# Key and query loads in 1.5 KB rows, a turn of two tokens at a time, and work moved from VectorE to ScalarE, in a sparse-attention and Fourier kernel

## The chip, the cores and the metric

The kernel runs on one core of one Trainium2 chip, everything in float32. The metric is device time in microseconds (us), the median of the runs of one kernel. A run is "fast" when it is not more than 1.5% above the fastest of the same kernel; all runs used here are fast, except the single run of e1, whose state is unknown and whose time is not used. A ratio is the mean time of one kernel's fast runs over the mean of the fast runs of the kernel before in the same rounds on the same chip, so it is not quite the ratio of the medians that stand beside it. An interval is a 95% interval. PE is TensorE, DVE VectorE, ACT ScalarE, POOL GpSimd.

## The reference

Four batches, eight heads of 64 columns, 768 tokens. Each query sees the keys less than 16 tokens away, and 24 block summaries (the largest key and the mean value of each block of 32). The result goes through a two-dimensional Fourier transform and a channel part:

```python
k_sum = k.reshape(B, H, nb, 32, D).max(axis=3);  v_sum = v.reshape(B, H, nb, 32, D).mean(axis=3)
# softmax over [q.k / 8 where |i - j| < 16 , q.k_sum / 8 + log 32], times [v, v_sum]
x = attn_out.transpose(0, 2, 1, 3).reshape(B, S, 512)
u = x + np.real(np.fft.fft(np.fft.fft(x, axis=1), axis=2))
un = (u - mean(u)) / np.sqrt(var(u) + 1e-6)
out = u + np.maximum(un @ w_ch1, 0.0) @ w_ch2        # 512 -> 2048 -> 512
```

## The kernel before

The parts that the change touches. Two heads make a pair. Keys and queries of a pair are loaded head by head, one token of 64 columns (256 B) per row, then turned on PE so that the 128 partitions hold the columns of the two heads and the free axis holds the tokens:

```python
qn, kn = (apool.tile([P, NST, 2, D], FP, tag="nat", bufs=4, ...) for n in "qk")
for dst, src in ((kn, k), (qn, q)):
    for e in range(2):
        nc.sync.dma_start(out=dst[:, :, e, :], in_=src[b, 2 * g + e].rearrange("(t p) d -> p t d", p=P))
...
for src, dst in ((kn, kt[:, W:W + S]), (qn, qt)):
    for h in range(2):
        ps = abank([P, HT, P], ...)                      # one PSUM bank, HT = 3
        for i in range(HT):
            nc.tensor.transpose(ps[:, i, :], src[:, HT * h + i].rearrange("p e d -> p (e d)"), ident)
        nc.scalar.copy(out=dst[:, S2 * h:S2 * (h + 1)], in_=ps.rearrange("p i c -> p (i c)"))
```

In the Fourier part y is the first product; its copies, then mx (second product), statistics, normalisation and the turn of u follow, before the first channel product hx:

```python
nc.scalar.copy(out=ty[:, g, par:S2:2], in_=y[:, 0:F2])
nc.vector.tensor_copy(out=tr[:, g, par:S2:2], in_=ps[:, F2:0:-1])     # the reversed copy
...                                                                   # mx, statistics, 4 Newton steps
nc.vector.tensor_scalar(out=un[:, t, :], in0=x[:, t, :], scalar1=stat[:, i, 0:1], scalar2=y[:, i:i + 1],
                        op0=SUB, op1=ALU.mult)
...                                                                   # transposes into ps
(nc.scalar.copy if t % 2 else nc.vector.tensor_copy)(out=u[:, half:half + 3:2, :, P * i:P * (i + 1)], in_=ps)
```

The rectifier of the channel part is `nc.vector.tensor_scalar(out=t, in0=t, scalar1=0.0, ..., op0=ALU.max)`. Attention of batch b + 1 runs interleaved with the Fourier and channel part of batch b, so its turns stand in the same engine queues.

## Time and profile before

930.12 us, median of 3 runs (928.45 to 930.68). The prediction below shows the stages; here are the totals of the profile page (engine, busy us, share of the span, instructions):

```profile
PE 829.2 (89%) x6386; PEld 618.3 (67%) x6386; DVE 530.3 (57%) x1158; ACT 168.8 (18%) x349; POOL 147.4 (16%) x142
```

And the timeline of ACT beside the Fourier products of batch 1, start and duration in us. It shows a pair's turn copies: two of keys in 0.87 us and two of queries in 0.88 us (about 0.48 each):

```profile
361.90 0.87 ACT L591 COPY kt<-qk 128x384 f32<-128x384 f32 x2
362.64 0.88 ACT L591 COPY qt<-qk 128x384 f32<-128x384 f32 x2
363.87 0.34 ACT L792 COPY big<-y 128x192 f32<-128x192 f32 x1 [0.34 <-PE y L786]
```

For the comparison of stages I use one landmark, the start of the first y product of each batch, from the timeline: 80.4, 350.6, 549.0 and 744.6 us here, end 929.2. The stages between them are called batch 0's attention (80.4 us), batch 0 (270.2), batch 1 (198.4), batch 2 (195.6) and batch 3 (184.6). The "turn" of a batch is the time from its first y to its first hx: 38.7 us in batch 1, 38.9 in batch 2.

### The profile page before, as it was taken

What the parts mean: (1) busy time and instruction counts of PE and PEld (TensorE: products, weight loads), DVE (VectorE), ACT (ScalarE), POOL (GpSimd) and SP (SyncE); (2) the same over time, 40 slices, a digit from 0 to 9 for tenths busy, and PEclk for the clock granted to TensorE, in tenths of its full rate; (3) what the DMA queues carried; (4) which work ended last, traced back from release to release, by engine and by line L of the source; (5) the groups of instructions that cost most, each with busy time, mean ns of one, the idle gap of its engine ahead of it and who ended that gap; (6) DMA issues with size and microseconds to landing.
All of it is one profiled execution on the core that took longest, in us unless ns stands there. A gap on an engine that the chain in (4) does not pass through costs nothing.

```text
span 929.2 us, 15289 instructions
## 1 busy us (share of the span) xinstructions
PE 829.2 (89%) x6386; PEld 618.3 (67%) x6386; DVE 530.3 (57%) x1158; ACT 168.8 (18%) x349; POOL 147.4 (16%) x142
## 2 busy tenths in 40 slices
PE   4778748687886799999999999999999997999997
PEld 3656634466753588657875888668857875587586
DVE  1366986799368964935423937635327556352252
ACT  2222312432023102221112012220021011200200
POOL 2230625567056700020000000000000000000000
PEclk9777859989898999999999999999999998999999
DMA  9995791777926508826162147321051161213101
GB/s 187 178 189 164 236 178 62 219 228 218 163 76 244 199 35 287 151 97 147 35 206 78 57 150 232 86 80 41 27 197 60 46 261 54 105 41 153 45 24 48
DMA packets 127917, 122.76 MB, mean 132 GB/s; under 512 B 102912, under 2 KB 111328, under 8 KB 127840
## 3 DMA queue, kind: packets, MB, share of 16 engines
q1 hardware_dynamic: 127296, 121.14, 46.9%
q8 instruction: 52, 0.85, 0.4%
q10 hardware_dynamic: 544, 0.56, 0.2%
q14 instruction: 25, 0.20, 0.1%
HBM read 100.71 MB, written 20.97 MB: 131 GB/s over the span
## 4 chain that ended last, share of the span: by engine, by line
PE 68%; DVE 20%; DMA 4%; POOL 3%; issue 3%; SPq 2%; ACT 1%; DVEq 0%; ACTq 0%; POOLq 0%
PE ox L906 17%; PE hx L863 15%; PE oz L906 8%; PE hz L863 7%; PE oy L906 4%; PE hy L863 4%; PE y L786 3%; DMA raw<-in_moe_w_ch_dram 2%; DVE cvt L688 2%; POOL w L529 2%; DVE cvt L693 2%; PE sc L606 2%; DVE cvt L691 2%; DVE x L526 2%; DVE cvt L687 2%
## 5 line engine op out<-in xcount | busy, mean ns | idle before, releaser
L863 PE MATMUL hx<-u,w 128*128 128x384 f32 x512 | 189.2, 500 | 15.5 <-ACT h L876 6.0
L863 PEld LDWEIGHTS hx<-u,w 128*128 128x128 f32 x512 | 97.9, 195 | 85.8 <-ACT h L876 8.9
L906 PE MATMUL ox<-w,h 128*128 128x256 f32 x384 | 93.9, 393 | 8.4 <-DVE x L526 7.9
L863 PE MATMUL hz<-u,w 128*128 128x384 f32 x256 | 96.6, 498 | 4.7 <-ACT h L878 4.7
L906 PE MATMUL ox<-w,s 128*128 128x256 f32 x384 | 92.8, 384 | 4.0 <-DVE x L526 3.5
L906 PE MATMUL oz<-w,s 128*128 128x256 f32 x384 | 93.0, 384 | 2.6 <-DVE s L526 2.6
L906 PEld LDWEIGHTS ox<-w,h 128*128 128x128 f32 x384 | 75.4, 197 | 22.8 <-DVE x L526 9.1
L906 PEld LDWEIGHTS ox<-w,s 128*128 128x128 f32 x384 | 72.0, 191 | 16.3 <-DVE x L526 5.6
L526 DVE TENSOR_TENSOR x<-ox,x 128x256 f32<-128x256 f32 x96 | 40.4, 422 | 74.2 <-PE ox L906 74.2
L906 PEld LDWEIGHTS oz<-w,s 128*128 128x128 f32 x384 | 73.3, 192 | 13.1 <-DVE s L526 2.9
L863 PEld LDWEIGHTS hz<-u,w 128*128 128x128 f32 x256 | 49.8, 195 | 40.3 <-POOL vb L529 5.3
L529 POOL TENSOR_TENSOR w<-cvt 128x512 f32<-128x512 f32 x32 | 43.6, 1364 | 133.2 <-DVE cvt L693 72.5
L529 POOL TENSOR_TENSOR w<-w 128x256 f32<-128x256 f32 x64 | 56.2, 893 | 3.1
L526 DVE TENSOR_TENSOR h<-hy,h 128x384 f32<-128x384 f32 x32 | 17.8, 555 | 67.5 <-PE hy L863 67.5
L526 DVE TENSOR_TENSOR h<-hx,h 128x384 f32<-128x384 f32 x32 | 17.8, 555 | 56.1 <-PE hx L863 56.0
L863 PE MATMUL hy<-u,w 128*128 128x384 f32 x128 | 46.5, 486 | 0.0
L906 PE MATMUL oy<-w,h 128*128 128x256 f32 x192 | 46.0, 380 | 0.3 <-POOL w L529 0.3
L606 PEld LDWEIGHTS sc<-qt,kt 64*64 64x64 f32 x1536 | 33.7, 157 | 12.7 <-issue 8.6
L606 PE MATMUL sc<-qt,kt 64*64 64x32 f32 x1536 | 36.7, 239 | 6.0 <-issue 3.7
L906 PEld LDWEIGHTS oy<-w,h 128*128 128x128 f32 x192 | 36.5, 191 | 5.8 <-POOL w L529 0.7
L867 DVE TENSOR_SCALAR h<-h 128x384 f32<-128x384 f32 x96 | 38.7, 404 | 2.9
L526 DVE TENSOR_TENSOR s<-h 128x512 f32<-128x512 f32 x48 | 39.2, 816 | 0.2
(92 smaller groups left out, 1043.3 us busy)
## 6 DMA issues: line engine op xcount, KB each, us to landing
w<-dw SPq DMA_DIRECT2D x48, 896.0 KB, 5.6
raw<-in_moe_w_ch_dram SPq DMA_DIRECT2D x32, 512.0 KB, 5.1
dw<-w SPq DMA_DIRECT2D x16, 896.0 KB, 4.3
vw<-in_v_dram SPq DMA_DIRECT2D x62, 192.0 KB, 5.7
kn<-in_k_dram SPq DMA_DIRECT2D x32, 192.0 KB, 5.3
qn<-in_q_dram SPq DMA_DIRECT2D x32, 192.0 KB, 5.2
vb<-in_v_dram SPq DMA_DIRECT2D x16, 384.0 KB, 6.3
out_dram<-x SPq DMA_DIRECT2D x24, 256.0 KB, 2.0
```

What stands on the lines that cost most here:

```text
L526: nc.vector.tensor_tensor(out=out, in0=in0, in1=in1, op=op)
L529: nc.gpsimd.tensor_tensor(out=out, in0=in0, in1=in1, op=op)
L606: nc.tensor.matmul(ps[h][r:r + 64, i, :], kt[rows, o:o + 64], qt[rows, o:o + BLOCK], start=True, stop=True)
L687: nc.vector.tensor_scalar(out=ex, in0=high, scalar1=0x7FF00000, scalar2=None, op0=ALU.bitwise_and)
L688: nc.vector.tensor_scalar(out=man, in0=high, scalar1=0x000FFFFF, scalar2=None, op0=ALU.bitwise_and)
L691: nc.vector.scalar_tensor_tensor(out=ex, in0=high, scalar=-(1 << 31), in1=ex, op0=ALU.bitwise_and, op1=ALU.bitwise_or)
L693: nc.vector.scalar_tensor_tensor(out=tmp[:, 1, :], in0=low, scalar=2.0 ** -52, in1=tmp[:, 1, :], op0=ALU.mult, op1=ALU.add)
L786: nc.tensor.matmul(y, fgs[par][:, st, P * g:P * (g + 1)], fs[par][:, g % 2, st, :], start=(st == 0), stop=(st == HT - 1))
L863: nc.tensor.matmul(ps, w[:, a, kk, :], u[:, r, kk, :], start=start and kk == 0, stop=stop and kk == 1, skip_group_check=True)
L867: nc.vector.tensor_scalar(out=t, in0=t, scalar1=0.0, scalar2=None, op0=ALU.max)
L906: nc.tensor.matmul(ps, left[a][:, n, :], wt[2, b, j][:, r, :], start=start and n == 0, stop=stop and n == NC - 1, skip_group_check=True)
```

## The change

Its intent: longer rows for the loads; less work on DVE, which is busy in batch 0; less arithmetic in the inverse square root. The long row holds six tokens of one head, so a transpose of 128 columns yields two tokens of one head; the copies out of PSUM have to put the even and the odd token back in order, half the partitions each.

```diff
-        for dst, src in ((kn, k), (qn, q)):
-            for e in range(2):
-                nc.sync.dma_start(out=dst[:, :, e, :], in_=src[b, 2 * g + e].rearrange("(t p) d -> p t d", p=P))
+            nc.sync.dma_start(out=dst, in_=src[b, 2 * g:2 * g + 2].rearrange("e (p t) d -> p e (t d)", p=P))
@@ turn
-            for h in range(2):
-                    nc.tensor.transpose(ps[:, i, :], src[:, HT * h + i].rearrange("p e d -> p (e d)"), ident)
-                nc.scalar.copy(out=dst[:, S2 * h:S2 * (h + 1)], in_=ps.rearrange("p i c -> p (i c)"))
+            for e in range(2):
+                    nc.tensor.transpose(ps[:, i, :], src[:, e, P * i:P * (i + 1)], ident)
+                to = dst[D * e:D * (e + 1)].rearrange("d (p i two) -> d two i p", i=HT, two=2)
+                for par in range(2):
+                    nc.scalar.copy(out=to[:, par], in_=ps[D * par:D * (par + 1)])
@@ copies, normalisation, rectifier
-                nc.vector.tensor_copy(out=tr[:, g, par:S2:2], in_=ps[:, F2:0:-1])
+                nc.scalar.copy(out=tr[:, g, par:S2:2], in_=ps[:, F2:0:-1])
-            for _ in range(4):                       # four small instructions each
+            for _ in range(3):                       # three each, by scalar_tensor_tensor
-            nc.vector.tensor_scalar(out=un[:, t, :], ... op0=SUB, op1=ALU.mult)
+            nc.scalar.activation(out=un[:, t, :], in_=x[:, t, :], func=AF.Identity, bias=shift[:, i:i + 1],
+                                 scale=y[:, i:i + 1])
-            (nc.scalar.copy if t % 2 else nc.vector.tensor_copy)(
-                out=u[:, half:half + 3:2, :, P * i:P * (i + 1)], in_=ps)
+            nc.scalar.copy(out=u[:, half:half + 3:2, :, P * i:P * (i + 1)], in_=ps)
-                    nc.vector.tensor_scalar(out=t, in0=t, scalar1=0.0, scalar2=None, op0=ALU.max)
+                    nc.scalar.activation(out=t, in_=t, func=AF.Relu)
```

Cut: the product of the attention with its reciprocal, two instructions made one.

More of the change, by code (lines that the diff above doesn't have):

```diff
@@ L534, in load @@
     def load(b, g):
-        qn, kn = (apool.tile([P, NST, 2, D], FP, tag="nat", bufs=4, name=f"{n}n_{b}_{g}") for n in "qk")
+        qn, kn = (apool.tile([P, 2, NST * D], FP, tag="nat", bufs=4, name=f"{n}n_{b}_{g}") for n in "qk")
         for dst, src in ((kn, k), (qn, q)):
-            for e in range(2):
-                nc.sync.dma_start(out=dst[:, :, e, :], in_=src[b, 2 * g + e].rearrange("(t p) d -> p t d", p=P))
+            nc.sync.dma_start(out=dst, in_=src[b, 2 * g:2 * g + 2].rearrange("e (p t) d -> p e (t d)", p=P))
         nat[b, g] = qn, kn
@@ L586, in prepare @@
         for src, dst in ((kn, kt[:, W:W + S]), (qn, qt)):
-            for h in range(2):
-                ps = abank([P, HT, P], f"qk_{b}_{g}_{h}")
+            for e in range(2):
+                ps = abank([P, HT, P], f"qk_{b}_{g}_{e}")
                 for i in range(HT):
-                    nc.tensor.transpose(ps[:, i, :], src[:, HT * h + i].rearrange("p e d -> p (e d)"), ident)
-                nc.scalar.copy(out=dst[:, S2 * h:S2 * (h + 1)], in_=ps.rearrange("p i c -> p (i c)"))
+                    nc.tensor.transpose(ps[:, i, :], src[:, e, P * i:P * (i + 1)], ident)
+                to = dst[D * e:D * (e + 1)].rearrange("d (p i two) -> d two i p", i=HT, two=2)
+                for par in range(2):
+                    nc.scalar.copy(out=to[:, par], in_=ps[D * par:D * (par + 1)])
         nc.vector.tensor_reduce(out=km[:, 0:nb], in_=kt[:, W:W + S].rearrange("p (n f) -> p n f", f=BLOCK),
@@ L647, in values @@
             nc.vector.reciprocal(out=rc, in_=av[r][:, :, D])
-            for h in range(2):
-                ts, c = slice(HT * h, HT * (h + 1)), P * g + D * (r ^ h)
-                tt(x[:, ts, c:c + D], av[r][:, ts, 0:D], rc[:, ts, None].to_broadcast([P, HT, D]), ALU.mult)
+            xo = x[:, 0, P * g + D * r:P * g + D * (r + 1)]
+            xo = bass.AP(xo.tensor, xo.offset, [list(xo.ap[0]), [HT * DM + D * (1 - 2 * r), 2], [DM, HT], [1, D]])
+            tt(xo, av[r].rearrange("p (h t) d -> p h t d", h=2)[:, :, :, 0:D],
+               rc.rearrange("p (h t) -> p h t", h=2)[:, :, :, None].to_broadcast([P, 2, HT, D]), ALU.mult)
     x_of = {}
@@ L822, in gen_fourier @@
                                     op0=ALU.mult, op1=ADD)
-            for _ in range(4):
-                tt(z, y, y, ALU.mult)
+            for _ in range(3):
+                nc.vector.scalar_tensor_tensor(out=z, in0=y, scalar=-0.5, in1=y, op0=ALU.mult, op1=ALU.mult)
                 tt(z, z, var, ALU.mult)
-                nc.vector.tensor_scalar(out=z, in0=z, scalar1=-0.5, scalar2=1.5, op0=ALU.mult, op1=ADD)
-                tt(y, y, z, ALU.mult)
-            norms.append((stat, y))
+                nc.vector.scalar_tensor_tensor(out=y, in0=z, scalar=1.5, in1=y, op0=ADD, op1=ALU.mult)
+            nc.vector.scalar_tensor_tensor(out=z, in0=stat[:, :, 0], scalar=-1.0, in1=y, op0=ALU.mult, op1=ALU.mult)
+            norms.append((y, z))
         for t in range(NST):
             half, i = divmod(t, HT)
-            stat, y = norms[half]
-            nc.vector.tensor_scalar(out=un[:, t, :], in0=x[:, t, :], scalar1=stat[:, i, 0:1], scalar2=y[:, i:i + 1],
-                                    op0=SUB, op1=ALU.mult)
+            y, shift = norms[half]
+            nc.scalar.activation(out=un[:, t, :], in_=x[:, t, :], func=AF.Identity, bias=shift[:, i:i + 1],
+                                 scale=y[:, i:i + 1])
             ps = bank([P, 2, 2, P], f"unt_{b}_{t}")
```

## The prediction

> **What bounds the kernel now.** I read the totals first, then engine busy time by stretch, then the chain that ended last in the first 70 us and in 70 to 355 us, then groups by shape.
>
> The kernel before, busy time of each engine in five stretches (span, then busy us and instruction count of PE, PEld, DVE, ACT, POOL, then granted TensorE clock, DMA share, GB/s):
>
> ```profile
> 0.00:70.00 70.00, 46.21 (x1106) 37.11 (x1114) 26.34 (x70) 18.66 (x40) 17.86 (x21) 0.82 1.06 185
> 70.00:355.00 285.00, 227.14 (x1544) 164.87 (x1525) 219.20 (x391) 69.43 (x130) 123.69 (x115) 0.86 0.61 169
> 355.00:550.00 195.00, 191.27 (x1502) 143.53 (x1495) 104.00 (x251) 30.89 (x69) 5.86 (x6) 1.00 0.45 124
> 550.00:745.00 195.00, 193.14 (x1584) 144.33 (x1583) 102.04 (x256) 29.98 (x67) 0.00 (x0) 1.00 0.33 106
> 745.00:929.20 184.20, 171.43 (x692) 128.47 (x690) 78.72 (x193) 19.81 (x43) 0.00 (x0) 0.97 0.24 92
> ```
>
> Three regimes. In the first 70 us (attention of batch 0) DMA is full. From 70 to 355 us (batch 0's Fourier and channel part, with weights converted beside it) nothing is full on average, but DVE is the largest non-PE load, and two narrower stretches, 184:235 (DVE 51.00 of 51) and 280:326 (43.85 of 46), are DVE-bound. From 355 us PE is full at full clock: batches 1 and 2 have 3.7 and 1.9 us of PE idle; only batch 3, with no attention beside it, has 12.8 us. So most of the change can pay only before 355 us.
>
> The chain that ended last, cut to 0 to 70 us (start, duration, what):
>
> ```profile
> 3.04 2.88 SPq L538
> ...
> 9.71 6.38 DMA vb<-in_v_dram
> ...
> 35.92 2.43 SPq L538
> 38.40 6.52 DMA qn<-in_q_dram
> ...
> 54.28 2.29 issue
> ```
>
> L538 is the key and query load. Its issues (SPq) are 17.8% of these 70 us and waiting for its data another 9.3%: 12.5 + 6.5 = 19 us. The same chain in 70 to 355 us is 136 us DVE, 90 PE, 23 DMA, 21 POOL and only 6 ACT (summed from the pieces shown).
>
> Durations used below, from the groups by shape:
>
> ```profile
> L867 DVE TENSOR_SCALAR h<-h 128x384 f32<-128x384 f32 x96 | 38.7, 404 | 2.9
> L833 DVE TENSOR_SCALAR big<-x,stat,norm 128x512 f32<-128x512 f32 x24 | 12.4, 548 | 0.1
> L689 ACT ACTIVATE cvt<-cvt,rebias 128x512 int32<-128x512 int32 x32 | 23.1, 722 | 82.7 <-DVE cvt L687 82.6
> L690 ACT ACTIVATE cvt<-cvt 128x512 f32<-128x512 int32 x32 | 20.0, 626 | 7.3 <-DVE cvt L688 5.0
> L878 ACT COPY h<-hz 128x384 f32<-128x384 f32 x32 | 15.3, 478 | 19.8 <-PE hz L863 19.8
> ```
>
> They give ACT's costs: about 480 ns for 384 columns from PSUM (the turn copies, L591, have 480 and 494), 626 for 512 from SBUF, and 96 more with one per-partition operand. The copies of u (L838) have 585 for 512 columns from PSUM.
>
> **What the Trainium skill says.** "ScalarE: Activation LUTs", section "What ACT_TABLE_LOAD costs": each per-partition pointer operand adds about 93 ns; here L689 against L690 shows 96, it agrees. "DMA: Bandwidth & Descriptors", section "Specifications": 512 B is the least transfer for line rate. The trace agrees in direction: four loads of 192 KB in 256 B rows are issued in 5.24 us (about 150 GB/s), while a weight reload in rows of some KB moved 430 to 459 GB/s. "PSUM — Partial Sum Buffer", section "Engine vs sequencer instructions": ScalarE's queue is a strict FIFO. It agrees: at 280 us PE idles 3.97 us for the copy of L876, because ACT stood at a conversion that waited for a weight load. "Perfetto Trace Analysis", section "Optimizing Scalar/DVE Operations": GpSimd and DVE share an SBUF read port, which a two-port DVE instruction holds. It agrees: the same L688 takes 0.42 us alone and 1.41 while POOL runs.
>
> **Part 1, loads.** Keys and queries are 32 + 32 loads of 192 KB, 12.6 MB in 49152 rows of 256 B. They become 32 loads of 393 KB in 8192 rows of 1.5 KB. One pair of heads now takes four issues of about 1.3 us (33.64 to 39.3 us: 5.6 us). At some 330 GB/s (my estimate, between the two measured rates) 786 KB take 2.4 us: about 3.2 us saved each. At the start the value-sum load vb, issued at 8.93 us behind eight small loads, should go out near 3 us and land 5 to 6 us earlier, and the chain runs through it. After that the period of one pair of heads is about 11 us (scores at 38.8, 49.3, 58.2), set by the queue; without it the PE and ACT work is 8 to 9 us. Five further pairs, minus 2 each, make 10. Together minus 15 to 16 us.
>
> **Part 2, the turn.** 64 copies of 128 partitions become 128 copies of 64 partitions. Width does not shorten them, columns do, and a copy with stride two (L792, 192 columns in 334 ns) lies on the same line as the dense one. So 28.5 us becomes 128 x 0.48 = 61, or 3.9 us instead of 1.95 for each pair. In the first stage vs and av take banks which these copies free, so about 1 us more for each of the first few pairs: plus 3. Parts 1 and 2 net: minus 12 to 13.
>
> **Part 3, DVE to ACT.** Off DVE: 96 rectifiers (38.7), 24 normalisations (12.4), 12 copies of u (8.3), 32 reversed copies (11.3): 71 us. On to ACT: 96 x about 0.52 = 50, 24 x (0.626 + 2 x 0.096) = 20, 12 x 0.585 = 7, 32 x 0.334 = 11. ACT goes from 169 to about 290 us, DVE from 530 to about 450.
>
> On the path this splits by stage. In batch 0 (70 to 355 us) the moved instructions are 12.8 (rectifiers), 3.1, 2.1 and 3.4 us, about 21 us of 219. Direct appearances on the chain are about 6 us, and DVE is about half the chain, so I count 9 to 10 us. ACT is a FIFO there, with conversions that wait for DVE and DMA among the rectifiers, so I give 3 back. Net with Part 4: minus 9.
>
> In the full-PE stage one product is 1.29 us. Laying one j by hand: Y's sum ends on DVE 0.83 us after Y's product, ACT's rectifier then runs 0.52, and the next X is ready to be copied 1.35 after that product. The rectifier ends just before it. ACT then has about 3.5 us of work in 9.03: no stall, no gain.
>
> **Part 4, Newton and normalisation.** Each of 8 chains goes from 16 small instructions to 10, of 0.13 to 0.2 us: about 1 us. It counts where PE waits, before the turn of u: batch 0 (inside the 9) and batch 3, where PE waits 4.03 + 2.72 us. There ACT's six normalisations and six copies, 6 x 0.82 + 6 x 0.585 = 8.4 us in series, take over from DVE: I count minus 2. In batches 1 and 2 ACT's order puts, between the first normalisation and the last copy of u, also two exponentials, one more, and eight turn copies: 4.9 + 3.5 + 1.4 + 3.8 = 13.6 us in series, which by hand puts the first channel product about 2 us later than now: plus 4 for both.
>
> **Part 5, value products.** 64 of 350 ns become 32 of about 555 (as the sums of 128x384 from PSUM): about 1 us off DVE, nothing on the path.
>
> **Sum.** 930 - 12.5 - 9 - 2 + 4 = 910.5; I put 909, as the shared port is relieved as well.
>
> **Rivals.** (a) ACT becomes the bound in the Fourier-to-channel turn of every batch and blocks the conversions in batch 0: plus 10 instead of minus 7 there, only the load gain stays, 918 to 928. For it: the strict order, and the 3.97 us stall above. Against: ACT is 18% busy now and about 32% after. (b) The load gain is hidden: after the first 70 us the weight pipeline (DMA raw, 23 us of chain) starts earlier but waits for the same POOL and DVE work, and value windows in 256 B rows still fill the queue: 920. Against: the chain enters the weight stage through the folds, which follow the last values. (c) Both stages gain fully: lighter DMA shortens raw loads (5 to 6 us each, four on the chain) and removes instruction waits such as the 2.29 us "issue": 890 to 895.
>
> **Range and chances.** The terms have errors of about 6 us (loads), 8 (batch 0) and 4 (turns), added as independent: 11. 8 in 10 is about 1.4 times that: 892 to 926. The 2% line is 911.5, only 2 us from my centre; I lean to faster because (c) has several independent ways: 0.57, 0.41, 0.02.
>
> **What would show it.** Right: the first Fourier product (y, at 80.4 us now) near 67 us; batch 1's first y near 332 instead of 350.8; ACT about 290 us and DVE about 450; rectifiers near 520 ns on ACT; batches 1 and 2 no shorter than now. Wrong: PE idle before hx with ACT as releaser for over 3 us in batches 1 and 2; rectifiers delaying the copies of X in the full-PE stage; or turn copies well over 0.5 us.

## The result, and the profile after

958.1 us, median of 4 runs (953.12 to 960.99), against 930.4 (928.45 to 934.05) for the kernel before in the same rounds: ratio 1.0287, interval 1.0233 to 1.0341. The change makes the kernel slower by 2.9%. The prediction, 909 us and 892 to 926, is wrong, in direction too.

The totals of the page after, and its DMA line:

```profile
PE 850.2 (89%) x6386; PEld 627.4 (66%) x6386; DVE 448.5 (47%) x914; ACT 326.7 (34%) x577; POOL 144.5 (15%) x142
...
DMA packets 86445, 122.76 MB, mean 132 GB/s; under 512 B 53248, under 2 KB 69856, under 8 KB 86368
```

DVE fell to 448.5, as predicted (about 450). ACT is at 326.7 instead of the predicted 290: 37 us too much, the first trace of the cause. PE does the same 6386 instructions in 21 us more busy time.

Engine busy time by stretch (columns as in the prediction's first fence):

```profile
0.00:70.00 70.00, 51.83 (x1034) 39.09 (x1034) 23.40 (x58) 43.86 (x59) 16.47 (x21) 0.78 0.99 202
70.00:355.00 285.00, 233.57 (x1627) 169.39 (x1630) 194.35 (x334) 110.98 (x201) 122.04 (x115) 0.86 0.59 174
355.00:550.00 195.00, 184.13 (x1427) 135.44 (x1420) 82.70 (x186) 67.46 (x116) 6.00 (x6) 0.97 0.37 109
550.00:745.00 195.00, 184.26 (x1505) 134.29 (x1505) 73.74 (x170) 64.57 (x120) 0.00 (x0) 0.96 0.32 103
745.00:951.30 206.30, 196.44 (x800) 149.19 (x799) 74.29 (x168) 39.81 (x84) 0.00 (x0) 0.97 0.23 86
```

In the third and fourth stretch PE was full before (191.27 and 193.14 us of 195). Now it is idle for 11 us in each, and the granted clock is 0.97 and 0.96 instead of 1.00. ACT is busy for a third of these stretches only: it is not at its limit there, and yet something waits.

The groups by shape (line, engine, operation, out<-in, count | busy us, mean ns | idle before):

```profile
L594 ACT COPY qt<-qk 64x384 f32<-64x384 f32 x64 | 53.9, 842 | 1.1
L594 ACT COPY kt<-qk 64x384 f32<-64x384 f32 x64 | 53.7, 840 | 4.9 <-PE qk L591 4.0
L870 ACT ACTIVATE h<-h 128x384 f32<-128x384 f32 x96 | 49.9, 522 | 115.9 <-DVE h L526 115.8
```

Rectifiers (522 ns) are as predicted, and so are the normalisations, whose group has a mean of 812 ns (0.626 + 2 x 0.096 = 0.818 predicted; a single one of 0.81 us stands in the chain further down). The turn copies are not: 0.84 us each instead of 0.48. They take 107.6 us of ACT instead of 61.

The chain that ended last in the first 70 us (start, duration, what; pieces of under 0.05 us are left out here and below) now goes through ACT where it went through loads:

```profile
40.46 0.87 ACT kt L594
...
43.04 0.83 ACT kt L594
43.88 0.84 ACT qt L594
44.73 0.84 ACT qt L594
45.61 1.63 PE av L641 x80
47.25 1.60 PE av L646 x12
48.85 1.09 PE sc L609 x33
```

Of the chain in these 70 us ACT's kt and qt have 38%. The scores of successive pairs (sc) start at 35.4, 48.9 and 62.5: a pair takes 13.5 us. In the kernel before the scores of four successive pairs start at 27.6, 37.0, 49.3 and 58.2: 10.2 us in the mean.

The chain in the turn of batch 1:

```profile
354.72 0.82 PE ss L623 x8
355.56 0.49 ACT psum L625
356.06 0.81 ACT kt L594
...
361.96 0.82 ACT qt L594
363.19 0.70 PE mx L810 x2
...
377.56 0.81 ACT big L837
...
382.20 0.47 ACT u L842
...
383.54 0.71 ACT kt L594
...
389.36 0.82 ACT qt L594
390.20 0.82 ACT big L837
391.06 1.12 PE unt L841 x4
```

Eight turn copies of the next batch's attention (6.7 us) stand in ACT's queue ahead of the last copies of y, which mx waits for; and eight more (6.6 us) stand between the fourth and the fifth normalisation (big), which the transposes of u wait for. The turn takes 49.2 us in batch 1 instead of 38.7 and 52.0 in batch 2 instead of 38.9.

All stages, from first y to first y (us; one profiled execution each). I include the runs of the next section that the argument needs:

| kernel | attention of batch 0 | batch 0 | batch 1 | batch 2 | batch 3 | turns of batches 1, 2 |
|---|---|---|---|---|---|---|
| before | 80.4 | 270.2 | 198.4 | 195.6 | 184.6 | 38.7, 38.9 |
| after | 83.0 | 261.5 | 210.9 | 212.5 | 183.4 | 49.2, 52.0 |
| e2, copies at step two | 78.4 | 258.8 | 205.1 | 203.4 | 182.4 | 43.9, 43.9 |
| e3, old loads and turn | 80.3 | 267.7 | 200.4 | 198.3 | 182.8 | 40.4, 40.0 |
| e5, loads, 128 short copies | 80.6 | 265.2 | 199.3 | 196.9 | 184.6 | 39.9, 39.9 |
| e8, e2 less normalisation | 79.2 | 254.4 | 198.7 | 197.6 | 183.4 | 39.5, 39.4 |
| e13, half the loads | 72.1 | 259.7 | 200.7 | 195.6 | 184.6 | 41.6, 38.9 |
| e16, best | 79.7 | 260.9 | 199.0 | 196.0 | 182.3 | 38.3, 38.3 |
| e17, loads, 64 short copies | 77.2 | 258.7 | 198.1 | 195.6 | 184.0 | 39.0, 38.9 |

The kernel of e16 was profiled twice (it is that of e11): batch 0 took 255.8 us in one profile and 260.9 in the other. So a difference of 5 us in that column, between two single profiles, is not a finding. The granted clock in that stage was 0.91 in the short one and 0.89 in the long one, and it is a rival in every comparison of this column: 0.88 before and in e5, 0.90 in e17, 0.92 in e8.

### The profile page after: what moved, and what is told of

The parts are those of the page before. It is cut to its first block, busy times and chain, and to the rows that moved or that the text cites. A ratio compares the mean times of both kernels' runs of the same rounds, so it can differ in the third digit from the quotient of the medians.

```text
span 951.3 us, 15247 instructions
## 1 busy us (share of the span) xinstructions
PE 850.2 (89%) x6386; PEld 627.4 (66%) x6386; DVE 448.5 (47%) x914; ACT 326.7 (34%) x577; POOL 144.5 (15%) x142
## 2 busy tenths in 40 slices
DMA packets 86445, 122.76 MB, mean 129 GB/s; under 512 B 53248, under 2 KB 69856, under 8 KB 86368
## 4 chain that ended last, share of the span: by engine, by line
PE 69%; ACT 12%; DVE 11%; DMA 4%; issue 2%; POOL 1%; SPq 1%; DVEq 0%; POOLq 0%; ACTq 0%
PE ox L909 16%; PE hx L866 16%; PE oz L909 8%; PE hz L866 7%; ACT kt L594 5%; PE hy L866 4%; PE oy L909 4%; PE sc L609 3%; PE y L790 3%; ACT qt L594 3%; DMA raw<-in_moe_w_ch_dram 3%; PE av L646 2%; DVE cvt L697 2%; ACT big L837 2%; DVE cvt L692 2%
## 5 line engine op out<-in xcount | busy, mean ns | idle before, releaser
L866 PE MATMUL hx<-u,w 128*128 128x384 f32 x512 | 195.3, 514 | 23.9 <-DVE h L526 11.0
L909 PE MATMUL ox<-w,h 128*128 128x256 f32 x384 | 90.4, 383 | 2.1 <-DVE x L526 2.1
L870 ACT ACTIVATE h<-h 128x384 f32<-128x384 f32 x96 | 49.9, 522 | 115.9 <-DVE h L526 115.8
L909 PEld LDWEIGHTS ox<-w,h 128*128 128x128 f32 x384 | 73.7, 193 | 15.5 <-DVE x L526 3.3
L526 DVE TENSOR_TENSOR x<-ox,x 128x256 f32<-128x256 f32 x96 | 40.2, 423 | 69.7 <-PE ox L909 69.5
L796 ACT COPY big<-y 128x192 f32<-128x192 f32 x32 | 10.7, 334 | 130.9 <-PE y L790 130.9
L594 ACT COPY kt<-qk 64x384 f32<-64x384 f32 x64 | 53.7, 840 | 4.9 <-PE qk L591 4.0
L594 ACT COPY qt<-qk 64x384 f32<-64x384 f32 x64 | 53.9, 842 | 1.1
L873 ACT COPY h<-hx 128x384 f32<-128x384 f32 x32 | 15.2, 476 | 108.6 <-PE hx L866 92.8
```

Source lines behind the costliest of these rows:

```text
L526: nc.vector.tensor_tensor(out=out, in0=in0, in1=in1, op=op)
L594: nc.scalar.copy(out=to[:, par], in_=ps[D * par:D * (par + 1)])
L866: nc.tensor.matmul(ps, w[:, a, kk, :], u[:, r, kk, :], start=start and kk == 0, stop=stop and kk == 1, skip_group_check=True)
L870: nc.scalar.activation(out=t, in_=t, func=AF.Relu)
L909: nc.tensor.matmul(ps, left[a][:, n, :], wt[2, b, j][:, r, :], start=start and n == 0, stop=stop and n == NC - 1, skip_group_check=True)
```

## The experiments

Theory A: the turn copies write SBUF at a step of 24 B (the third index of the output, p, steps six tokens), and this makes them long; that one term explains the loss. Rival B: ScalarE's strict order, with normalisation and the copies of u in it, costs in the turns whatever the length of the turn copies. Rival C: it is the 64 partitions, or the crossing from upper to lower partitions, that makes the copies long.

### e1_strides: probe copies

```diff
+    pps = bank([P, S2], "pps");  nc.vector.memset(pps, 1.0)
+    for _ in range(4):
+        nc.scalar.copy(out=pr[:, 0:384], in_=pps)
+        nc.scalar.copy(out=pr[0:64, 0:384], in_=pps[0:64])          # then pps[64:128]
+        nc.scalar.copy(out=pr[0:64, 0:768:2], in_=pps[0:64])        # then steps 3, 4, 5, 6, 8
+        ...                                                         # 128 partitions step 6; VectorE steps 1, 6
```

> The kernel before plus four rounds of probe copies at its end, each of 384 float32 columns from PSUM to SBUF, with one thing varied: 128 or 64 partitions, straight or crossed (upper 64 to lower 64), and the step of the write (1, 2, 3, 4, 5, 6, 8 elements). Theory A (the step of 24 bytes makes the turn copies long): 64 partitions dense and crossed stay at 0.48 us, step 2 at 0.48, and somewhere between step 3 and step 6 the time rises to 0.84 us. Rival C (half the partitions, or the crossing, is what costs): the 64-partition copies are at 0.84 us whatever the step, and 128 partitions with step 6 stay at 0.48. For DVE I have no figure; if step is a matter of the SBUF write, DVE shows it too.

The probes by line, in the order of the diff (ns min/median/max, first and last start, shapes). Though written at the end of the kernel's text, they ran from 3.9 to 44 us, before the Fourier part:

```profile
L956 ACT COPY probe<-pps x4: 479/480/486, 3.9 to 36.6; 128x384 f32<-128x384 f32 x4
L957 ACT COPY probe<-pps x4: 472/473/483, 4.4 to 37.1; 64x384 f32<-64x384 f32 x4
L958 ACT COPY probe<-pps x4: 476/476/477, 4.9 to 37.6; 64x384 f32<-64x384 f32 x4
L959 ACT COPY probe<-pps x4: 487/494/501, 8.5 to 38.1; 64x384 f32<-64x384 f32 x4
L960 ACT COPY probe<-pps x4: 662/670/683, 9.3 to 38.6; 64x384 f32<-64x384 f32 x4
L961 ACT COPY probe<-pps x4: 824/830/832, 10.0 to 39.3; 64x384 f32<-64x384 f32 x4
...
L963 ACT COPY probe<-pps x4: 819/820/842, 12.1 to 41.0; 64x384 f32<-64x384 f32 x4
...
L966 DVE COPY probe<-pps x4: 549/550/550, 14.7 to 43.6; 64x384 f32<-64x384 f32 x4
L967 DVE COPY probe<-pps x4: 825/833/835, 16.4 to 44.4; 64x384 f32<-64x384 f32 x4
```

Half the partitions cost nothing (L957) and crossing costs nothing (L958): rival C falls. Step two (L959) is nearly free, step three (L960) costs 0.2 us, step four and every larger one 0.82 to 0.84. With all 128 partitions step six took 836 ns as well. VectorE shows it too (L967). The Trainium skill has the rule, and the prediction did not look it up: "SBUF — State Buffer", section "Specifications (TRN2)", says that SBUF has 16-byte cachelines and needs at least two hits per line for full bandwidth. The runs agree: at step two two float32 elements fall in a line of 16 B, at step three four in three lines, from step four on one in a line. The page gives no figure for the penalty; here it is 0.83 - 0.48 = 0.35 us for 384 elements, about 0.9 ns each.

### e2_dense_copy: the changed kernel with copies at step two

```diff
-                ps = abank([P, HT, P], ...)
+                ps = abank([P, P, HT], ...)
-                    nc.tensor.transpose(ps[:, i, :], src[:, e, P * i:P * (i + 1)], ident)
+                    nc.tensor.transpose(ps[:, :, i], src[:, e, P * i:P * (i + 1)], ident)
-                    nc.scalar.copy(out=to[:, par], in_=ps[D * par:D * (par + 1)])
+                    nc.scalar.copy(out=dst[D * e:D * (e + 1), par:S:2],
+                                   in_=ps[D * par:D * (par + 1)].rearrange("d p i -> d (p i)"))
```

> The changed kernel with one thing undone: the transposes write PSUM at a step of three elements, so that each turn copy writes SBUF at a step of two. Same loads, same number of copies, everything else of the change kept. Theory A (one mis-sized term, 128 copies at 0.84 instead of 0.48 us): copies at 0.48 us, ACT about 281 us, first Fourier product near 68 to 72 us, time 905 to 920. Rival B (ScalarE's strict order with normalisation and the copies of u in it is what costs in batches 1 and 2, whatever the length of the turn copies): the first product comes early, but batches 1 and 2 stay at 206 to 211 us each and the time is 935 to 948. A third way: the transposes themselves become longer by writing PSUM at a step, then PE busy rises by more than 5 us.

930.71 us (930.03 to 933.43), ratio 1.0013 (0.998 to 1.0046). The copies take 0.50 us and ACT is at 283.8: the step was worth 1.0287 - 1.0013 = 2.7%, 25.5 us (the two intervals make some 6 us of uncertainty). But the time is 930, not 905 to 920: Theory A is right about the copies and wrong in that they explain everything. The turns stay at 43.9 us in both batches. The third way fails too: PE busy is 838.2 us, not more than in the changed kernel (850.2), and the transposes did not become longer (median 273 ns and 109 ns from start to start, as in both kernels). The transposes and the copies of the keys in e2:

```profile
L591 PE MATMUL qk<-ident,kn x96: 272/273/473, 4.9 to 615.5; 128*128 128x128 f32 x96
...
L593 ACT COPY kt<-qk x64: 485/501/532, 5.8 to 617.0; 64x384 f32<-64x384 f32 x64
```

### e3_old_turn and e4_turn_alone: the two halves of the change

e3 is the changed kernel with the loads and the turn of before; e4 is the kernel before with the loads and the turn of the change.

```diff
 e3: the hunks "load" and "turn" of the change undone
 e4: only the hunks "load" and "turn" of the change done
```

> The changed kernel with the loads and the turn of the kernel before (256-byte rows, 64 copies of 0.48 us); only the moves to ScalarE, the shorter Newton chain and the single value product remain. Theory A: it keeps the 9 us of batch 0 and about 2 of batch 3 and loses at most 4 in batches 1 and 2: 917 to 925, ratio 0.985 to 0.995. Rival B: batches 1 and 2 are 6 us or more longer each although the turn copies are short: 930 to 942.

> The kernel before with the new loads and the new turn alone; rectifiers, normalisation and copies of u stay where they were. Theory A: the turn alone carries the loss. Batch 0's attention ends 2 to 3 us later than before, batches 1 and 2 lose 8 to 13 us each: 945 to 960, ratio 1.015 to 1.03. Rival B: ScalarE has room for 128 long copies when nothing else was moved to it, so batches 1 and 2 stay within 3 us of before and the time is 930 to 938.

e3: 925.74 us (921.84 to 931.2), ratio 0.9936 (0.9899 to 0.9972); e4: 954.08 (949.49 to 954.39), 1.024 (1.02 to 1.028). Both ratios fall where Theory A put them (e3's median is 0.7 us above its 925), so the loads with their turn carry the loss. But e3 gains at the low end of what was expected, which e8 explains.

### e5_dense_turn_alone and e6_twice_copies: the loads and the number of copies

e5 is e4 with copies at step two. e6 is the kernel before, loads untouched, with each turn copy made as two:

```diff
 e6
-                nc.scalar.copy(out=dst[:, S2 * h:S2 * (h + 1)], in_=ps.rearrange("p i c -> p (i c)"))
+                for e in range(2):
+                    nc.scalar.copy(out=dst[D * e:D * (e + 1), S2 * h:S2 * (h + 1)],
+                                   in_=ps[D * e:D * (e + 1)].rearrange("p i c -> p (i c)"))
```

> The kernel before with the long-row loads and the new turn, but its copies written at a step of two elements (0.50 us). This is what the prediction thought parts 1 and 2 were: 128 copies of 0.48. If the load gain of 12 to 13 us exists, 917 to 921. If the load gain is hidden (the rival of the prediction), and the doubled copies only cost: 929 to 936. In the run with everything of the change and such copies, the first Fourier product came at 78.5 instead of 80.4 us, so I expect the second.

> The kernel before, its loads untouched, with each of its 64 turn copies made as two of 64 partitions, dense, no partition crossed. It prices the doubled number of copies by itself, and against the run with long rows and the same number of copies it prices the loads. If 64 further copies of 0.48 us cost what the prediction said (3 us in the first stage, 4 in batches 1 and 2): 935 to 938. If ScalarE has room for them: 929 to 932. If they cost more (5 us in each of the two turns and 3 us in each later pair of the first stage): 942 to 950; then the load gain is real and eaten by them.

e5: 928.24 us (927.73 to 928.73), ratio 0.9976 (0.9947 to 1.0005), just below the second expectation. e6: 933.13 (932.61 to 934.72), 1.0027 (0.9998 to 1.0056). Between short and long rows with 128 short copies there are 0.5%, about 5 us. The doubled copies alone cost about 3 us on short rows. This looked like a load gain of 5 us, a third of the predicted; e17 shows that this reading was too low. Against e4 (1.024), e5 also prices the step without the other moves: 2.6%, 24.6 us, as e2 did with them.

### e7_split_copies: half of the copies on VectorE

```diff
-                    nc.scalar.copy(out=dst[...], in_=ps[...])
+                    (nc.vector.tensor_copy if par else nc.scalar.copy)(out=dst[...], in_=ps[...])
```

> The changed kernel with copies written at a step of two, and half of them (the odd tokens) on the vector engine, so that two engines turn a pair side by side. If ScalarE's four copies in a row per tensor are what ate the load gain: first Fourier product at 70 to 74 us, turns of batches 1 and 2 (first Fourier product to first channel product) back to 39 to 41 us from 44 and 41.5, time 910 to 922. If the first stage is bounded by something else (value loads, folds on the vector engine, PE at a low clock): first product at 77 us or later and 925 to 932.

938.66 us (936.45 to 941.26), ratio 1.0098: neither. The turns of batches 1 and 2 did come back to 40.6 and 40.7 us, but batch 0's own turn became 60.6 us instead of 57.0 and its attention ended at 80.9: there VectorE is the loaded engine. That this load is the reason was not tested by itself: e9 below, which splits only beside batches 1 and 2, gained nothing either.

### e8_norm_back: normalisation and half of the copies of u back on VectorE

```diff
 from e2
-            nc.scalar.activation(out=un[:, t, :], in_=x[:, t, :], func=AF.Identity, bias=shift[...], scale=y[...])
+            nc.vector.tensor_scalar(out=un[:, t, :], in0=x[:, t, :], scalar1=y[...], scalar2=shift[...],
+                                    op0=ALU.mult, op1=ADD)
-            nc.scalar.copy(out=u[...], in_=ps)
+            (nc.scalar.copy if t % 2 else nc.vector.tensor_copy)(out=u[...], in_=ps)
```

> The changed kernel with copies written at a step of two, and the normalisation and half of the copies of u back on the vector engine as before. Rival B (ScalarE's strict order in the turn costs on its own): the turns of batches 1 and 2 come back from 44 and 41.5 us to 39 to 40 us, time 4 to 7 us shorter than with them on ScalarE (931 in the earlier call), 923 to 927. If the turn copies alone make the turn longer: no change beyond 2 us, and batch 3 loses about 1 us.

914.75 us (913.89 to 919.12), ratio 0.9843 (0.9804 to 0.9883). Against e2's 1.0013 that is 1.7%, 15.8 us: rival B holds as well, and for more than it claimed. ACT's timeline in e2, turn of batch 1:

```profile
373.51 2.01 ACT L593 COPY kt<-qk 64x384 f32<-64x384 f32 x4
375.54 2.05 ACT L593 COPY qt<-qk 64x384 f32<-64x384 f32 x4
377.60 1.52 ACT L837 ACTIVATE big<-x,norm 128x512 f32<-128x512 f32 x2
```

DVE's timeline there has the values that these last two normalisations need:

```profile
370.56 0.16 DVE L831 SCALAR_TENSOR_TENSOR norm<-stat,norm 128x3 f32<-128x3 f32 x1
375.02 0.29 DVE L526 TENSOR_TENSOR vs<-vs,half 128x128 f32<-128x128 f32 x1 [4.31 <-PE vs L631]
```

They are ready at 370.7 us, and DVE then stands idle for 4.31 us, while ACT works off what is ahead of the normalisations in its queue until 377.6. In e8 the DVE does them at once:

```profile
370.46 0.15 DVE L831 SCALAR_TENSOR_TENSOR norm<-stat,norm 128x3 f32<-128x3 f32 x1
370.65 1.46 DVE L837 TENSOR_SCALAR big<-x,norm 128x512 f32<-128x512 f32 x3
```

Counted from the first y (337.3 and 333.6), these last normalisations begin after 40.3 us in e2 and after 37.0 in e8; the turn is 43.9 and 39.5. The same move, on an engine that was idle, was not free: it queued behind work of another stage.

### e12_scale_back: only the normalisation back

```diff
 from e2: the first two hunk lines of e8, the copies of u stay on ScalarE
```

> The version with step-two copies (931 us) with only the 24 normalisations back on the vector engine; the copies of u stay all on ScalarE. Normalisation and half the copies of u together were worth 16 us. If it is the 0.81 us normalisations in ScalarE's strict order: 914 to 918. If it is the copies of u, which take turns between two engines in the kernel before: 926 to 931.

918.49 us (917.04 to 919.57), ratio 0.985 (0.9821 to 0.9879), beside e8's 0.9843. The normalisation is the cost; the copies of u make no difference that these runs resolve.

### e9_split_late and e10_relu_back: two edits of e8

```diff
 e9
+                    (nc.vector.tensor_copy if par and b > 1 else nc.scalar.copy)(out=dst[...], in_=ps[...])
 e10
-                    nc.scalar.activation(out=t, in_=t, func=AF.Relu)
+                    nc.vector.tensor_scalar(out=t, in0=t, scalar1=0.0, scalar2=None, op0=ALU.max)
```

> The version with step-two copies and normalisation back on the vector engine (914.8 us), with the odd half of the turn copies on the vector engine too, but for batches 2 and 3 alone, whose turns fall beside batches 1 and 2, where the vector engine is not the bound. If the eight turn copies in ScalarE's queue still hold back the copies of y by 3 to 5 us per batch: 908 to 912. If the vector engine, which splits everywhere made worse by 8 us, loses as much in the turn as ScalarE gains: 914 to 919.

> The 914.8 us version with the 96 rectifiers back on the vector engine. If the rectifiers are what shortened batch 0's Fourier and channel part (254.4 instead of 265.2 us with loads and turn alone): 922 to 927, with batch 0's part at 262 to 266. If the reversed copies of y and the shorter Newton chain did it: 913 to 917.

e9: 919.55 us (917.53 to 921.89), ratio 0.9855 (0.9827 to 0.9884), no gain (its turns took 40.2 and 40.1 us, e8's 39.5 and 39.4). e10: 921.16 (918.23 to 922.73), 0.9869 (0.9835 to 0.9903); e8 had 0.9843. The rectifiers may be worth 2 us; the intervals overlap, and e10 lies between its two expectations.

### e11_short_rows and e14_short_twice: the loads in the best setting

e11 is e8 with the loads and the 64 copies of before; e14 is e11 with each copy made as two, as in e6.

```diff
 e11: from e8, the hunks "load" and "turn" undone
 e14: from e11, the edit of e6
```

> The 914.8 us version with the loads and the 64 turn copies of the kernel before: of the change only rectifiers, reversed copies, the shorter Newton chain and the single product remain. If the loads are worth about 5 us net of their copies only in price of 128 copies (3 us), as the two runs with 128 copies say: 916 to 920. If loads and moves only work together (loads alone 2 us, moves with normalisation on ScalarE 6 us): 922 to 926. If the new loads are worth nothing here: 911 to 915, and the best version keeps the old turn.

> The best version with the old loads (915.7), with each turn copy made as two of 64 partitions: the same number and length of copies as the best version with long rows (914.8), so that the two differ by the loads alone. If loads are worth what the two runs without other moves say (5 us): 918 to 921. If nothing: 914 to 916.

e11: 915.73 us (914.91 to 916.14), ratio 0.9819 (0.9792 to 0.9846). e14: 917.42 (915.56 to 923.12), 0.9855 (0.9822 to 0.9888). Long rows with 128 short copies (e8, 0.9843) and short rows with 64 (e11) or 128 (e14) are the same within the intervals. e11 against e3 is the price of the normalisation with 64 copies: 0.9936 - 0.9819 = 1.2%, 11 us.

### e15_reversed_back and e16_best

```diff
 e15: from e11
-                nc.scalar.copy(out=tr[:, g, par:S2:2], in_=ps[:, F2:0:-1])
+                nc.vector.tensor_copy(out=tr[:, g, par:S2:2], in_=ps[:, F2:0:-1])
 e16: e11 once more
```

> The best version with the old loads, with the 32 reversed copies of y back on the vector engine: rectifiers, the shorter Newton chain and the single product alone remain of the change. If the copies of y in one queue lengthen the turn (they wait behind turn copies on ScalarE): 912 to 914. If they relieve the vector engine in batch 0: 917 to 920.

> The best version with the old loads once more, in five rounds, as the control of the two before it and to settle whether it beats the kernel before by 2%: 914 to 917, ratio 0.979 to 0.985.

e15: 918.59 us (917.25 to 919.49), ratio 0.9852 (0.9823 to 0.988). e16: 915.0 (911.43 to 919.59), 0.9813 (0.9782 to 0.9843). The reversed copies on ScalarE seem to help by 3 to 4 us; the intervals just touch. e16 is the best correct version: rectifiers and reversed copies on ScalarE, the shorter Newton chain, one value product, and nothing else of the change. It beats the kernel before by 1.9% and the changed kernel by 4.6% (0.9813 / 1.0287). Its totals:

```profile
PE 826.6 (90%) x6386; PEld 613.2 (67%) x6386; DVE 471.4 (51%) x950; ACT 224.8 (24%) x477; POOL 144.1 (16%) x142
```

### e13_half_loads: is the first stage bound by loads? (wrong result)

```diff
-        for dst, src in ((kn, k), (qn, q)):
+        for dst, src in ((kn, k),):                                    # the queries are turned from kn
```

> Wrong on purpose: the kernel before with the query loads left out (the queries are turned from the key tile), so that half of the 256-byte rows and half of the issues are gone and everything else stays. The prediction read 19 us of loads in the first 70 us of the chain as what the stage is bound by. If so, the first Fourier product (80.4 us) comes at 68 to 72 us and the time is 918 to 922. If the loads only just come ahead of other work that is as long (PE at a low clock with waits for issue, then the folds on the vector engine): 77 to 80 us in the first stage, and a gain only in batch 0's later part, 924 to 928.

914.12 us (908.77 to 914.78), ratio 0.9786 (0.9746 to 0.9826). The first y comes at 72.1 us instead of 80.4, just above the first expectation's 68 to 72, so the stage does depend on loads (the time lies below both expectations). Of the chain, the load of the value sums (vb):

```profile
5.27 6.44 DMA vb<-in_v_dram
```

The value-sum load starts at 5.3 and lands at 11.7 us, 4.4 us earlier than in the kernel before: here the transfers ahead of it are gone, not only their issues.

### e17_long_rows_64 and e18_norm_back_64: long rows without doubled copies (wrong result)

Each bank is copied whole, which mixes tokens of the two heads but keeps number, size and step of a good turn. A correct form of this would transpose the same token of both heads, from two pieces of a row.

```diff
 e17: from e5;  e18: from e8
-                for par in range(2):
-                    nc.scalar.copy(out=dst[D * e:D * (e + 1), par:S:2], in_=ps[D * par:D * (par + 1)]...)
+                nc.scalar.copy(out=dst[:, e:S:2], in_=ps.rearrange("d p i -> d (p i)"))
```

> Wrong on purpose: the kernel before with the long-row loads and 64 turn copies of 128 partitions at a step of two (each bank is copied whole, so tokens of the two heads are mixed and the result is wrong, but number, size and step of the copies are those of a good turn). Against the kernel before it differs in the row length alone. If the load gain is real and was eaten by the 64 further copies: first Fourier product at 72 to 76 us and 918 to 923 us. If the row length gains nothing because the same bytes pass through the same queues (the load of the value sums landed 9 us after its issue instead of 6): 79 to 81 us and 925 to 930.

> Wrong on purpose in the same way: the version with normalisation back on the vector engine and long rows (914.8), with 64 whole copies instead of 128. It tells what the change could have been worth at most, had the token-pair turn not doubled the copies. If the copies eat the load gain: 903 to 909. If the row length gains nothing: 911 to 916, as its twin with short rows and 64 copies (915.0).

e17: 916.75 us (915.26 to 919.55), ratio 0.9861 (0.9837 to 0.9885), a little below the first expectation's 918 to 923; its first y, at 77.2 us, fits neither. The long rows alone, which come with half as many load issues, are worth 12.9 us. e5, with the same loads and 128 copies, had 0.9976: the doubled copies cost 10.7 us beside long rows, where they cost 3 beside short ones. e18: 910.61 (907.92 to 913.95), ratio 0.9791 (0.9763 to 0.9818): with everything that gained, long rows would be worth 0.2%, 2 us, over e16 (0.9813), which the intervals do not resolve. The gains do not add.

Where e17 gains is not where the prediction put it: 3.2 us in the first stage, 11.5 in batch 0, next to nothing after (one profile each; a part of the 11.5 can be the variation and the clock named under the table). The chain of its first stage:

```profile
4.17 10.67 DMA vb<-in_v_dram
...
51.10 3.66 DVE p L526 x2
```

The value-sum load is issued from 2.93 us on, as predicted (near 3), but then takes 10.67 us to land instead of 6.38: at 14.84, only 1.3 us earlier than before. And the two products p at 51.10 take 3.66 us; in the kernel before the same two took 1.03:

```profile
51.59 1.03 DVE L526 TENSOR_TENSOR p<-p,near 128x384 f32<-128x384 f32 x2 [0.81 <-ACT p L610]
```

The timeline of POOL in e17 says what they met:

```profile
50.44 2.35 POOL L529 TENSOR_TENSOR vb<-vb,vb 96x1024 f32<-96x1024 f32 x1 [14.37 <-DMA vb<-in_v_dram]
52.86 3.01 POOL L529 TENSOR_TENSOR vb<-vb 96x512 f32<-96x512 f32 x3
```

POOL's adds of the next value sums, released by the earlier load, now fall on these products; in the kernel before they began at 57.02 us. This is the shared port of the prediction's fourth citation, met at a new place: 2.6 us of the gain of this stage went there. About 1.2 us came back, because in the kernel before the same adds fell on the folds (sums on DVE) that follow: the first took 2.58 us there and 1.76 here, the next two together 2.19 and 1.82. The folds begin at 58.26 us here and at 59.74 before. Nor did the pairs come faster: the scores of the same four pairs start at 26.3, 35.1, 45.6 and 56.7 us, 10.1 us apart in the mean against 10.2; twice PE pauses for 2.5 us among them (at 35.4 and 46.3) and the profile shows nothing that it waited for. I have not traced the 11.5 us of batch 0 piece by piece. What DVE waited for raw weights from 80 to 345 us fell from 10.6 to 6.5 us, which is part of it.

## Why the prediction was wrong

A ladder of ratios, each against the kernel before of its own rounds and times 930 us: long rows alone (e17) 0.9861, -12.9 us; doubling the copies (e5) 0.9976, +10.7; rectifiers, reversed copies, Newton chain and single product (e8) 0.9843, -12.4; normalisation and copies of u to ScalarE (e2) 1.0013, +15.8; writing at a step of 24 B (the change) 1.0287, +25.5. Sum +26.7. Each rung is uncertain by 2 to 6 us, from the intervals of its two ratios. e17's rung rests on a kernel with a wrong result but the same work. The shares of the first three rungs depend on the order: moves first (e16, 0.9813) -17.4, then long rows (e18, 0.9791) -2.0, then doubled copies (e8) +4.8. The step's share does not: without the moves (e4 against e5) it is 24.6.

**Part 1, loads: size nearly right by luck, place wrong.** Predicted -15 to -16, all in the first stage; measured -12.9, of which about 3 are there. Both steps failed. The value-sum load should land 5 to 6 us earlier: it landed 1.3 us earlier, though issued 6 us earlier. That it waited for the transfer of the same bytes and not for their issue is what e13 suggests, where half of the key and query bytes are gone and it lands 4.4 us earlier. And a pair should take 2 us less: it took 10.1 us instead of 10.2. (The prediction read 11, from scores "at 38.8"; that is where they resume after a pause, the pair begins at 36.96.) The first Fourier product, predicted near 67 us, came at 77.2 even in e17; batch 1's first y, predicted near 332, came at 335.9. The gain came in batch 0, in the direction of the prediction's own rival (c). Rival (b), a hidden gain, is refuted by e17 for the kernel before; beside the moves (e18 against e16) only 2 us of the gain are left.

**Part 2, the turn: the step that failed first.** It says that a copy with stride two "lies on the same line as the dense one", and then "So 28.5 us becomes 128 x 0.48 = 61". Stride two is indeed nearly free (e1: 494 ns), but the change writes at stride six. I read the two parities as the step and overlooked that p steps over i and two, six tokens. Measured 107.6 us of ACT and 25.5 us of time. The prediction had named the sign: turn copies well over 0.5 us. "About 1 us more for each of the first few pairs: plus 3" holds for the first stage, as far as single profiles tell: 80.6 us in e5 against 77.2 in e17, and in e2's chain six of a pair's eight copies stand in a row. But the doubled copies cost 10.7 us beside long rows; the prediction had no term for batch 0, where the profiles put 6.5 us of it (not traced, and barely above the variation there); 2.5 are in batches 1 and 2.

**Part 3, the rectifiers and reversed copies: right.** Together with the Newton chain -12.4 measured. The prediction had -9 for batch 0, which includes the normalisation there, and -1.5 for the shared port. Rectifiers take 522 ns, and in the stretch of the full-PE stage that I read (616 to 634 us of the changed kernel) they end just before the next copy of X, as laid out by hand. DVE is at 448.5. Which of the pieces earns it is not settled: e10 and e15 give each 2 to 4 us, at the edge of their intervals.

**Part 4, normalisation on ScalarE: the second step that failed.** It was counted as -2 in batch 3 and +2 in each of batches 1 and 2. It cost 15.8 us with 128 copies and 11 with 64. ACT's 13.6 us in series, with eight turn copies among them, were right: in e2 14.3 us pass between the first normalisation and the end of the last copy of u, against 8.5 in the kernel before. What failed is the step from there to the first channel product "about 2 us later than now": it came 5.2 and 5.0 us later (43.9 against 38.7 and 38.9), and 4.4 and 4.5 of these went when DVE took the normalisation back (e8). The layout did not see that DVE, which had done this work, would stand idle while data ready at 370.7 us waited until 377.6. In the profiles of e2 and e8 batches 1 and 2 lose 6.4 and 5.8 us by it and batch 0 loses 4.4, where the prediction had counted a gain. With 64 copies the turns differ by 2 us (40.4 and 40.0 in e3, 38.3 and 38.3 in e16), and the rest seems to lie in batch 0 (267.7 us in e3, 260.9 and 255.8 in e16's two profiles). Rival (a) had named the strict order and its cost in every turn; I gave it too little weight because ACT's average was a third. Its sign, PE idle for ACT before hx for over 3 us, came one step earlier: in batch 1's turn of the changed kernel PE waits for ACT 3.4 us before mx and 3.3 us before the transposes of u (0.7 and 2.0 in e2). Batch 3 gained 1.2 us (predicted 2).

**Part 5:** not measured by itself; the single product took 553 ns as predicted (555). Two slips without effect: L688's "1.41 while POOL runs" is its piece of the chain (that instruction took 1.49 us, most beside POOL 0.94 to 0.99), and 1.4 times 11 is 15, where the range takes 17 on each side.

From the predicted -21 to the measured +26.7 there are 48 us: 25.5 are the write step, 13.8 the normalisation (15.8 instead of 2), 7.7 the doubled copies (10.7 instead of 3), 2.6 the loads (-12.9 instead of -15.5), and -1.9 the moves that paid (-12.4 instead of -9 and -1.5). The first three rungs' shares are those of this order of the ladder.

## What to carry to other kernels

Work out the step in bytes of the innermost index that an engine writes, after the whole rearrangement, before using a duration from a dense copy; if it exceeds 8 B for float32, let the producer write PSUM in an order that lets the copy write at 8 B or less, which cost the transposes nothing here. Work moved to an engine that is idle on average still takes its place in that engine's queue: look at what stands ahead of it at the moment when its input is ready. When a transfer is made cheaper, ask what its earlier end sets off, and whether the copies that were hidden beside it still are.

## What the Trainium skill lacked or had wrong

- "SBUF — State Buffer", "Specifications (TRN2)" has the rule of two hits per 16-byte line, but no figure, and it names neither engine nor direction; no page has a figure for the writes of ScalarE or VectorE (the one in "GPSIMD Engine Reference" is for GpSimd's reads). For writes from PSUM to SBUF: 384 float32 elements took 476 ns dense, 494 at 8 B, 670 at 12 B, 820 to 840 from 16 B on; VectorE 550 dense and 833 at 24 B. The same page's section "Door 1: The DMA port swizzle" says that a stride of up to four fp32 is free; a step of three already cost 41% more.
- "PSUM — Partial Sum Buffer", "Specifications (TRN2)" says that a non-contiguous access pattern slows matmuls significantly. Transposes that wrote PSUM at a step of 12 B took 273 ns in the median and started 109 ns apart, exactly as the contiguous ones, and copies that read the bank densely again took 0.50 us.
- "DMA: Bandwidth & Descriptors", "Specifications" gives 512 B as the least size for line rate. Rows of 1.5 KB for keys and queries moved 213 instead of 201 GB/s in the first stage (e2 against before), at a mean busy share of the DMA engines of 1.01; beside them ran value rows that stayed short (53248 packets under 512 B in the whole execution). What of this is the short rows' doing was not measured.
- None of the pages says what a position in ScalarE's queue costs: 24 normalisations of 0.54 us, moved to an engine that was busy for 18% of the span, cost 11 to 16 us.
